# Weight tiles of a retention and FFN kernel converted in pairs: twenty of 32 in operations of 1024 columns

## The chip, the cores and the metric

The kernel runs on one core of a Trainium2 chip. A core has five engines that run side by side, each in the order of its own program: TensorE (PE, matrix products), VectorE (DVE), ScalarE (ACT), GpSimd (POOL) and SyncE (SP, which here starts the DMA transfers). They wait for each other by semaphores. The metric is the time of one execution in microseconds (us).

## The reference

Eight batches of 576 tokens with eight heads of 64 go through a retention (attention with a decay in place of a softmax). Its output is the input x of a feed-forward layer with a rational function between two products:

```python
gamma = 1.0 - 2.0 ** (-5.0 - np.arange(H))
Dmat = np.where(rel >= 0, gamma[:, None, None] ** rel, 0.0)   # rel = i - j
ret = (scale * q @ k.T * Dmat) @ v
x = ret.transpose(0, 2, 1, 3).reshape(B * S, H * D)            # 4608 x 512
h = x @ w_in                                                    # 512 x 2048
P = a[0] + a[1] * h + a[2] * h2 + a[3] * h3
Q = 1.0 + abs(b[0]) * abs(h) + abs(b[1]) * h2
out = (P / (Q + 1e-06)) @ w_out                                 # 2048 x 512
```

w_in and w_out come as 64-bit floats, the rest as 32-bit ones.

## The kernel before

The tokens are cut into 36 units of 128, worked off in "visits" of 64x64 matmuls, and into nine blocks b of 512 for the feed-forward layer; its hidden columns into 16 tiles f of 128. A step is one (b, f). It runs `gemm1` (h{b}_{f} = x times a tile of w_in, 12 matmuls of 512 columns), the rational function on ScalarE and VectorE (tiles p, u, v, named p{b}_{f} and so on; in steps 8 to 20 u lies in a spare PSUM tile called free_at), the split of the result into g hi and g lo, and three or four steps later `gemm2` (acc += g times a tile of w_out, 12 matmuls). The order of steps is block 0 with f 0 to 7, block 1 with all 16, block 0 with f 8 to 15, then blocks 2 to 8. Twelve matmuls stand for four because each fp32 operand is a sum of a hi and a lo part, and three of the four products are taken.

Each of the 32 weight tiles (128 x 512, 16 of w_in called i0 to i15, 16 of w_out called o0 to o15) is converted from its 64 bits on the chip, in five instructions: on ScalarE c <- the high words of bits and bits <- the low words (both read every other 32-bit word), on VectorE an stt (scalar_tensor_tensor: shift and or) that joins them in c, on ScalarE w hi <- c, and on VectorE or GpSimd w lo = c - w hi. The tiles o0 to o3 lie in `held` tiles and are used whole at first; their w hi comes late, from step 7 on, and reads every other word of `held`.

PSUM (the memory that matmuls write) holds two buffers for h, so the gemm1 of step i+2 waits until the instruction p2 of step i (`ffn_p2`, on VectorE) has read the first h. The results of block 0's first half are moved out of PSUM by the two evictions o0_0 and o0_1 on ScalarE (1024 columns each), which the first gemm2 of block 1 waits for.

Everything is written out by hand and kept in that order on each engine: the lists FIRST0 to FIRST23, MID, DENSE, DENSE_ALONE and REST name the parts of a step in the order in which they are recorded (split0 to split3 are the four points at which conversions under way go on by one instruction, `start` begins new ones), and further lists say for every step or tile which engine does a part: VA and SCALES, SCALES_Q, LO, WLO. All recorded instructions bear the line number of the recording helper, L86, so that rows of the trace are told apart by the names of tiles.

Of the kernel before, what the change touches and what calls it, by code (L numbers as in the profile page):

```python
# [21 lines left out]
P = 128  # L22
# [15 lines left out]
FIRST0 = "gemm1 split0 start ffn_r visit split3 decay decay1 ffn_p ffn_q ffn_va ffn_v gemm2 ffn_p2 keep_hi add split1 keep_lo ffn_hi split2 ffn_lo scale_v fade scale_q ffn_q3".split()  # L38
FIRST1 = "gemm1 visit split1 ffn_r ffn_p decay scale_q keep_hi scale_v split0 ffn_p2 decay1 ffn_va add ffn_q split3 ffn_q3 start ffn_v ffn_hi split2 fade keep_lo gemm2 ffn_lo".split()
FIRST2 = "start ffn_hi gemm1 scale_q visit ffn_lo decay ffn_p keep_hi decay1 add split2 ffn_va ffn_p2 scale_v fade ffn_r ffn_q split3 gemm2 split1 ffn_v keep_lo ffn_q3 split0".split()  # L40
FIRST3 = "split3 gemm2 ffn_hi start gemm1 ffn_r visit decay split1 split0 ffn_p decay1 add scale_v keep_hi ffn_va ffn_q split2 scale_q ffn_v keep_lo ffn_q3 fade ffn_lo ffn_p2".split()
FIRST4 = "gemm1 split0 ffn_p gemm2 split3 ffn_p2 visit scale_q ffn_r ffn_va decay decay1 start keep_hi ffn_q split2 split1 ffn_hi ffn_q3 add fade ffn_v keep_lo scale_v ffn_lo".split()
FIRST5 = "scale_q ffn_hi gemm1 split3 scale_v visit split0 decay decay1 add start ffn_p gemm2 keep_hi ffn_r ffn_va split1 fade ffn_v ffn_q ffn_p2 ffn_q3 split2 ffn_lo keep_lo".split()
FIRST6 = "ffn_r gemm1 split0 split3 gemm2 ffn_p visit ffn_hi decay keep_hi scale_v split1 ffn_lo decay1 split2 start ffn_va add ffn_q fade ffn_q3 keep_lo ffn_v ffn_p2 scale_q".split()
FIRST7 = "scale_v ffn_hi start gemm1 ffn_p visit keep_hi split0 ffn_p2 ffn_va decay ffn_lo ffn_v gemm2 decay1 add split3 ffn_r ffn_q keep_lo ffn_q3 scale_q split1 split2 fade".split()
FIRST21 = "visit gemm1 gemm2 scale_v split1 decay decay1 ffn_p add keep_hi ffn_r ffn_va ffn_hi keep_lo start ffn_lo split2 ffn_p2 ffn_q ffn_q3 ffn_v split0 fade scale_q split3".split()
FIRST22 = "split1 scale_v visit gemm1 scale_q ffn_p keep_hi keep_lo decay ffn_va ffn_hi ffn_r start decay1 ffn_lo ffn_q gemm2 ffn_p2 split2 add split0 ffn_v fade ffn_q3 split3".split()
FIRST23 = "start split3 scale_q split2 gemm1 visit ffn_p ffn_hi ffn_r decay ffn_p2 ffn_q keep_hi split1 decay1 keep_lo ffn_q3 add ffn_va ffn_v split0 gemm2 scale_v fade ffn_lo".split()
MID = "split2 gemm1 start ffn_p split0 ffn_p2 ffn_r gemm2 ffn_hi ffn_va ffn_v ffn_q ffn_q3 ffn_lo split3 split1".split()
DENSE = "scale_q split0 gemm1 ffn_p ffn_hi visit keep_hi split2 decay ffn_va ffn_v scale_v decay1 split3 ffn_lo ffn_r ffn_q gemm2 ffn_q3 add ffn_p2 split1 fade keep_lo".split()  # L50
DENSE_ALONE = "split2 split0 gemm1 visit split1 gemm2 scale_q ffn_p ffn_r decay ffn_p2 keep_hi decay1 ffn_q add ffn_hi ffn_lo keep_lo fade split3 ffn_va ffn_v scale_v ffn_q3".split()
# [38 lines left out]
def retention_ffn(ctx: ExitStack, tc: tile.TileContext, qkv, w_in, w_out, consts, masks, out):  # L90
# [17 lines left out]
    cnv = ctx.enter_context(tc.tile_pool(name="cnv", bufs=4))  # L108
# [15 lines left out]
    def load_unit(n):  # L124


        late = 2 <= n < 6
        pools = [(wts, f"w{w}_{10 + n}") if late else (raw, "qk" if w == 0 else "kv") for w in range(2)]
        qk = pools[0][0].tile([P, 2, NPAIR, P], F32, tag=pools[0][1], name=f"qk{n}")
        nc.sync.dma_start(qk, qkv[n, :, 0:1024].rearrange("p (a g i) -> p a g i", a=2, g=NPAIR))  # L130
        kv = pools[1][0].tile([P, 2, H, D], F32, tag=pools[1][1], name=f"kv{n}")
# [30 lines left out]
    plain, held = {}, []  # L162
    step = -1

    def load_weight(k):

        bits[k] = wts.tile([P, DM], I64, tag=f"w{k[0]}_{k[1]}", name=f"bits{k[0]}_{k[1]}")
        nc.sync.dma_start(bits[k], (w_in, w_out)[k[0]][k[1]])

    def split_weight(k):  # L170


        nm = f"{k[0]}_{k[1]}"
# [22 lines left out]
        while late and step < PLAIN_TO + PLAIN.index(str(k[1])):  # L196
            yield
        w = wts.tile([P, 2, DM], F32R, tag=f"w{nm}", name=f"w{nm}")
        del bits[k]
        if late:  # L200
            cf = cf.rearrange("p (n a) -> p a n", a=2)
        halved = [w[:, i, :].rearrange("p (a n) -> p a n", a=2) if late else w[:, i, :] for i in range(2)]
# [377 lines left out]
    def gemm2(b, f, first, last):  # L580
# [42 lines left out]
    def put_last(b, t, acc):  # L623

        if t != 2:
            pool_, tag, n = (op, "o0", 2) if t == 0 else (cnv, "c", 1)
            lasts.append(pool_.tile([P, n, DM], F32, tag=tag, name=f"last{t}"))
# [3 lines left out]
        def store_rows(queue, a, tiles, o):  # L631
            queue.dma_start(rows[a][:, tiles], o[a::2])
# [107 lines left out]
    for i in range(len(steps) + lag(len(steps))):  # L740
# [28 lines left out]
        load_weights(2)  # L769
# [42 lines left out]
```

## Time and profile before

| | us |
|---|---|
| three runs | 866.65, 869.79, 869.87 (median 869.79) |
| the profiled execution | 866.07 |
| its span, from the first to the last instruction | 864.3 |
| TensorE busy | 844.1 (98%) |
| VectorE busy | 760.1 (88%) |
| ScalarE busy | 670.1 (78%) |
| GpSimd busy | 127.4 (15%) |

The busy times are sums over the whole span. The conversion of weights lies in the first fifth of it, where the shares are others; the rows below show them by stretch.

### The profile page before, as it was taken

Reading aid. Unit: us, or ns where it says so; the run is one execution under the profiler, and the core shown is the slowest. Engines: PE = TensorE matmul, PEld = TensorE weight load, DVE = VectorE, ACT = ScalarE, POOL = GpSimd, SP = SyncE. Lnnn points to the kernel's source line nnn. Section 1 sums busy time; section 2 is a strip of 40 time slices with the busy share of each in tenths; the row PEclk is TensorE's granted clock in tenths of the full one; section 3 lists DMA queues with packets and bytes.
Section 4 is the critical chain, followed back from the end, with each engine's and each line's share of the span. In section 5 each row is a group of like instructions: output and inputs, shape, how many; then the busy total and the mean of one; then the engine's idle time right before and its main releaser. Section 6 shows DMA issues by size and latency. Waiting matters only on the chain.

```text
span 864.3 us, 18728 instructions
## 1 busy us (share of the span) xinstructions
PE 844.1 (98%) x7574; PEld 727.1 (84%) x7574; DVE 760.1 (88%) x1222; ACT 670.1 (78%) x1234; POOL 127.4 (15%) x105
## 2 busy tenths in 40 slices
PE   8799899999999999999999999999999999999997
PEld 6667788888888888888888888888888888888886
DVE  4999989999988888888888888898888998888995
ACT  3998999997777778777877787778777787767774
POOL 4411344230001110111111110001111111000000
PEclk9999999999999999999999999999999999999999
DMA  9994000033111112111211121111201121001001
GB/s 343 358 351 188 1 2 0 2 135 112 38 71 41 50 50 99 50 50 50 98 50 50 49 99 50 49 49 47 77 31 46 50 99 50 1 2 49 1 1 49
DMA packets 20773, 64.54 MB, mean 75 GB/s; under 512 B 2512, under 2 KB 2640, under 8 KB 20688
## 3 DMA queue, kind: packets, MB, share of 16 engines
q1 hardware_dynamic: 20528, 63.10, 20.7%
q8 instruction: 59, 0.97, 0.5%
q14 instruction: 26, 0.21, 0.1%
q10 hardware_dynamic: 160, 0.26, 0.1%
HBM read 53.91 MB, written 9.44 MB: 73 GB/s over the span
## 4 chain that ended last, share of the span: by engine, by line
PE 87%; ACT 8%; issue 2%; DVE 2%; DMA 0%; POOL 0%; SPq 0%; DVEq 0%; ACTq 0%; POOLq 0%
PE acc L86 40%; PE h L86 39%; PE ps L86 4%; PE y L86 2%; ACT free_at L86 2%; ACT c L86 1%; PE psNone L86 1%; ACT p L86 1%; ACT w L86 1%; ACT g L86 1%; DMA qk<-in_qkv 0%; ACT v L86 0%; DVE kv L86 0%; PE ps_None L86 0%; DVE p L86 0%
## 5 line engine op out<-in xcount | busy, mean ns | idle before, releaser
L86 PE MATMUL acc<-w,g 128*128 128x512 f32 x1584 | 368.1, 382 | 2.9 <-ACT o L86 2.2
L86 PE MATMUL h<-xhi,w 128*128 128x512 f32 x1152 | 366.8, 380 | 2.6 <-DVE p L86 1.2
L86 PEld LDWEIGHTS acc<-w,g 128*128 128x128 f32 x1584 | 297.9, 190 | 47.2 <-ACT o L86 2.6
L86 PEld LDWEIGHTS h<-xhi,w 128*128 128x128 f32 x1152 | 217.7, 189 | 34.8 <-DVE p L86 1.6
L86 ACT ACTIVATE p<-h,const_sb 128x512 f32<-128x512 f32 x144 | 111.5, 774 | 160.0 <-PE h L86 159.8
L86 PE MATMUL h<-xlo,w 128*128 128x512 f32 x576 | 218.4, 379 | 1.0 <-DVE xlo L86 1.0
L86 DVE TENSOR_TENSOR p<-p,h 128x512 f32<-128x512 f32 x144 | 98.7, 685 | 50.6 <-ACT u L86 47.7
L86 PEld LDWEIGHTS h<-xlo,w 128*128 128x128 f32 x576 | 108.9, 189 | 17.1 <-DVE xlo L86 1.3
L86 DVE SCALAR_TENSOR_TENSOR p<-p,const_sb,h 128x512 f32<-128x512 f32 x144 | 107.4, 746 | 3.9
L86 POOL TENSOR_TENSOR S<-S,const_sb 128x256 f32<-128x256 f32 x32 | 37.3, 1166 | 462.3 <-DVE S L86 431.8
L86 ACT ACTIVATE v<-u,absb 128x512 f32<-128x512 f32 x128 | 102.6, 801 | 0.1
L86 DVE SCALAR_TENSOR_TENSOR p<-v,p 128x512 f32<-128x512 f32 x140 | 97.9, 700 | 3.7
L86 DVE SCALAR_TENSOR_TENSOR p<-p,const_sb,u 128x512 f32<-128x512 f32 x131 | 98.2, 749 | 0.5 <-ACT u L86 0.5
L86 DVE TENSOR_TENSOR v<-v,u 128x512 f32<-128x512 f32 x130 | 90.1, 693 | 1.7 <-ACT v L86 1.7
L86 DVE SCALAR_TENSOR_TENSOR v<-v,u 128x512 f32<-128x512 f32 x131 | 89.9, 686 | 0.0
L86 ACT ACTIVATE u<-u 128x512 f32<-128x512 f32 x131 | 82.8, 632 | 4.2
L86 ACT ACTIVATE g<-p 128x512 fp32r<-128x512 f32 x132 | 82.7, 626 | 3.3 <-DVE p L86 3.1
L86 ACT ACTIVATE u<-v 128x512 f32<-128x512 f32 x131 | 82.0, 626 | 1.8 <-DVE v L86 1.8
L86 DVE TENSOR_TENSOR g<-p,g 128x512 fp32r<-128x512 f32 x114 | 78.1, 685 | 0.7 <-ACT g L86 0.7
L86 ACT ACTIVATE u<-h 128x512 f32<-128x512 f32 x131 | 76.8, 586 | 1.0 <-DVE v L86 0.9
L86 ACT ACTIVATE kv<-kv,const_sb 128x64 f32<-128x64 f32 x224 | 56.2, 335 | 0.0
L86 POOL TENSOR_TENSOR qk<-qk,const_sb 128x512 f32<-128x512 f32 x32 | 43.7, 1366 | 45.0 <-DMA qk<-in_qkv 45.0
(95 smaller groups left out, 701.3 us busy)
## 6 DMA issues: line engine op xcount, KB each, us to landing
qk<-in_qkv SPq DMA_DIRECT2D x36, 512.0 KB, 4.2
kv<-in_qkv SPq DMA_DIRECT2D x32, 512.0 KB, 5.6
bits<-in_w_in SPq DMA_DIRECT2D x16, 512.0 KB, 9.0
bits<-in_w_out SPq DMA_DIRECT2D x16, 512.0 KB, 9.3
out<-o SPq DMA_DIRECT2D x28, 256.0 KB, 3.1
kv<-in_qkv SPq DMA_DIRECT2D x4, 256.0 KB, 7.2
out<-o SPq DMA_DIRECT2D x8, 128.0 KB, 2.1
out<-last SPq DMA_DIRECT2D x2, 256.0 KB, 2.4
```

The costliest lines, as they stand in the source:

```text
L86: return lambda *a, **k: self.tc.keep_in_program_order(method(*a, **k))
```

## The change

Twenty of the 32 tiles are converted two at a time: the list GROUPS names twelve single tiles (the first eleven, and o13, which stands between the last two pairs) and ten pairs. A pair is loaded into one tile of 128 x 2 x 512 and goes through c, bits and the stt in one instruction of 1024 columns each, and through w hi in one of 2 x 512; w lo stays one instruction a tile. The pool `cnv` has two buffers of 1024 columns instead of four of 512, and two single tiles share one. The loads are spread over the steps by a list LOADW instead of two a step, four early units are loaded into the space of the last four pairs, and the output of block 1 leaves from one tile of two halves. All the lists of order and of engines are new. TensorE's matmuls are the same; two visits (in steps 4 and 6) stand ahead of that step's gemm2 now.

```diff
-STARTS = "1 2 1 2 2 0 1 0 1 0 1 1 1 1 1 1 2 1 1 2 1 1 1 1".split()
+STARTS = "1 1 2 1 1 1 0 0 1 1 0 1 0 1 1 1 0 1 1 1 0 0 0 0".split()
+GROUPS = "i0 i1 i2 i3 o0 i4 o1 i5 o2 i6 o3 i7,o4 o5,o6 o7,i8 i9,i10 i11,o8 i12,o9 i13,o10 i14,o11 i15,o12 o13 o14,o15".split()
-MID = "split2 gemm1 start ffn_p split0 ffn_p2 ffn_r gemm2 ffn_hi ffn_va ffn_v ffn_q ffn_q3 ffn_lo split3 split1".split()
+MID = "split3 start gemm1 split0 split1 ffn_p ffn_p2 ffn_r ffn_hi ffn_va ffn_q ffn_v ffn_q3 split2 gemm2 ffn_lo".split()
+LOADW = "4 0 1 2 0 2 1 0 0 0 1 1 1 0 3 3 0 0 0 2".split()
...
-    cnv = ctx.enter_context(tc.tile_pool(name="cnv", bufs=4))
+    cnv = ctx.enter_context(tc.tile_pool(name="cnv", bufs=2))
...
+    def load_weight(g):
+
+        bits[g] = wts.tile([P, len(groups[g]), DM], I64, tag=f"w{g}", name=f"bits{g}")
+        for i, (w, f) in enumerate(groups[g]):
+            nc.sync.dma_start(bits[g][:, i], (w_in, w_out)[w][f])
...
-            c = cnv.tile([P, DM], I32, tag="c", name=f"c{nm}")
-            cf = c.bitcast(F32)
+            if n == 2 or not shared:
+                shared[:] = [cnv.tile([P, 2 * DM], F32, tag="c", name=f"c{g}")]
+                flat = shared[0][:, 0 : n * DM]
+                if n == 2:
+                    shared.clear()
+            else:
+                flat = shared.pop()[:, DM:]
+        c, cf = flat.bitcast(I32), flat.rearrange("p (f c) -> p f c", f=n)
-        act.activation(cf, high.bitcast(F32), AF.Prelu, scale=math.ldexp(1.0, -112), alpha=-math.ldexp(1.0, 32))
+        act.activation(flat, high.bitcast(F32), AF.Prelu, scale=math.ldexp(1.0, -112), alpha=-math.ldexp(1.0, 32))
         act.activation(packed, low.bitcast(U32), AF.Copy, scale=math.ldexp(7.49, -32))
...
-        act.activation(halved[0], cf, AF.Copy)
-        engine = dve if WLO[len(parts)] == "vector" else pool
-        engine.tensor_tensor(halved[1], cf, halved[0].bitcast(F32), ALU.subtract)
-        parts[k] = w
+        act.activation(whole[:, :, 0], cf, AF.Copy)
+        for i, k in enumerate(groups[g]):
+            engine = dve if WLO[len(parts)] == "vector" else pool
+            engine.tensor_tensor(whole[:, i, 1], cf[:, i], whole[:, i, 0].bitcast(F32), ALU.subtract)
+            parts[k] = both[:, i]
...
-        load_weights(2)
+        load_weights(int(LOADW[i]) if i < len(LOADW) else 0)
```

Where the lists move instructions is seen in the order of the engines' programs. The first place is ScalarE around the two evictions o0_0 and o0_1 (written o0_0_7 and o0_1_7; the last number of a name only tells tiles apart). Before:

```order
L86 ACTIVATE g1_0_1163<-p1_0_1050 128x512
L86 ACTIVATE w1_3_1171<-held1_414 128x512
L86 ACTIVATE c0_9_1192<-bits0_9_853 128x512
L86 ACTIVATE bits0_9_853<-bits0_9_853 128x512
L86 ACTIVATE p1_3_1196<-h1_3_1179,const_sb_95 128x512
L86 ACTIVATE free_at_1032<-h1_3_1179 128x512
L86 ACTIVATE free_at_1032<-v1_2_1143 128x512
L86 ACTIVATE free_at_1032<-free_at_1032 128x512
L86 ACTIVATE o0_0_7_1215<-acc0_0_0_670 128x1024
L86 ACTIVATE o0_1_7_1217<-acc0_0_1_671 128x1024
L86 ACTIVATE g1_1_1219<-p1_1_1090 128x512
```

The same place in the changed kernel, where c15 and bits15 are the c and bits of the pair i11,o8 (a group's number in GROUPS, counted from 0, stands in place of a tile's):

```order
L88 ACTIVATE g1_0_1121<-p1_0_1026 128x512
L88 ACTIVATE c15_1144<-bits15_867 128x1024
L88 ACTIVATE bits15_867<-bits15_867 128x1024
L88 ACTIVATE p1_3_1162<-h1_3_1147,const_sb_95 128x512
L88 ACTIVATE free_at_1000<-h1_3_1147 128x512
L88 ACTIVATE free_at_1000<-v1_2_1113 128x512
L88 ACTIVATE free_at_1000<-free_at_1000 128x512
L88 ACTIVATE g1_1_1169<-p1_1_1066 128x512
L88 ACTIVATE o0_0_7_1188<-acc0_0_0_670 128x1024
L88 ACTIVATE o0_1_7_1190<-acc0_0_1_671 128x1024
```

A pair stands where one tile stood, the late w hi (w1_3 before) has moved further ahead, and g1_1 has passed from behind the evictions to ahead of them.

The second place is VectorE at the end of the start, around the last xlo that the first gemm1 reads. Before:

```order
L86 TENSOR_TENSOR xlo0_194<-psNone_2_215,xhi0_193 128x4x128
L86 TENSOR_TENSOR S4_332<-S3_276,early_110 128x256
L86 TENSOR_TENSOR w0_1_340<-c0_1_271,w0_1_340 128x512
L86 TENSOR_TENSOR xlo0_194<-psNone_3_305,xhi0_193 128x4x128
L86 TENSOR_TENSOR qk4_244<-psNone_4_360,mask_sb_96 128x512
L86 TENSOR_TENSOR qk5_252<-qk5_252,const_sb_95 128x512
```

And in the changed kernel, where w0 is the tile i0 (w0_1 above is i1):

```order
L88 TENSOR_TENSOR xlo0_192<-psNone_2_213,xhi0_191 128x4x128
L88 TENSOR_TENSOR S4_326<-S3_271,early_110 128x256
L88 TENSOR_TENSOR w0_331<-c0_264,w0_331 128x512
L88 TENSOR_TENSOR xlo0_192<-psNone_3_300,xhi0_191 128x4x128
L88 TENSOR_TENSOR both4_242<-psNone_4_354,mask_sb_96 128x512
L88 TENSOR_TENSOR both5_249<-both5_249,const_sb_95 128x512
```

VectorE's w lo ahead of the last xlo is that of tile i0 now, and GpSimd does that of i1; before it was the other way round.

## Rows read from the trace of the kernel before

**Rows 1.** Stretches: busy time (and instructions) of each engine, clock, DMA share, GB/s.

```profile
40.00:73.00 33.00, 30.03 (x304) 19.89 (x295) 31.39 (x55) 30.25 (x55) 4.05 (x4) 1.00 0.94 359
73.50:98.80 25.30, 24.20 (x112) 20.66 (x110) 24.70 (x39) 24.67 (x39) 8.24 (x6) 1.00 0.09 32
98.80:153.20 54.40, 51.43 (x228) 44.11 (x228) 50.22 (x76) 53.48 (x85) 22.22 (x18) 0.97 0.00 1
176.00:850.00 674.00, 673.23 (x6052) 586.97 (x6051) 597.66 (x967) 508.56 (x969) 67.08 (x51) 1.00 0.16 54
```

The engines stand in the order PE, PE's weight loads, VectorE, ScalarE, GpSimd.

**Rows 2.** Waits of TensorE: us in total, times, longest.

```profile
PE ps L86 <- issue: 2.8, 1, 2.8
PE acc L86 <- ACT o L86: 2.2, 1, 2.2
...
PE h L86 <- DVE p L86: 1.2, 1, 1.2
...
PE h L86 <- DVE xlo L86: 1.0, 1, 1.0
PE h L86 <- DVE kv L86: 0.7, 1, 0.7
...
PE h L86 <- ACT v L86: 0.7, 1, 0.7
```

**Rows 3.** Stretch behind the wait for o (columns as in rows 1).

```profile
100.30:103.60 3.30, 3.30 (x9) 2.62 (x8) 3.27 (x5) 3.27 (x6) 1.28 (x1) 0.50 0.00 0
```

**Rows 4.** Timeline of TensorE: start, us, operation, idle before and its releaser.

```profile
92.36 2.75 PE L86 MATMUL acc<-w,g 128*128 128x512 f32 x12
...
99.91 4.54 PE L86 MATMUL acc<-w,g 128*128 128x512 f32 x12 [2.21 <-ACT o L86]
```

**Rows 5.** Timeline of ScalarE, pieces from p0_7 to behind o0_0.

```profile
74.35 0.76 ACT L86 ACTIVATE p<-h,const_sb 128x512 f32<-128x512 f32 x1
...
79.54 0.78 ACT L86 ACTIVATE p<-h,const_sb 128x512 f32<-128x512 f32 x1 [0.28 <-PE h L86]
...
87.33 0.78 ACT L86 ACTIVATE v<-free_at,absb 128x512 f32<-128x512 f32 x1
88.00 0.87 ACT L86 ACTIVATE w<-held 128x512 fp32r<-128x512 f32 x1
88.77 0.62 ACT L86 ACTIVATE w<-c 128x512 fp32r<-128x512 f32 x1
89.29 0.87 ACT L86 ACTIVATE c<-bits 128x512 f32<-128x512 f32 x1
90.19 0.89 ACT L86 ACTIVATE bits<-bits 128x512 int32<-128x512 uint32 x1
90.99 0.77 ACT L86 ACTIVATE p<-h,const_sb 128x512 f32<-128x512 f32 x1
...
98.84 1.94 ACT L86 ACTIVATE o<-acc 128x1024 f32<-128x1024 f32 x2
100.65 0.64 ACT L86 ACTIVATE g<-p 128x512 fp32r<-128x512 f32 x1
101.17 0.64 ACT L86 ACTIVATE w<-c 128x512 fp32r<-128x512 f32 x1
101.69 0.69 ACT L86 ACTIVATE c<-bits 128x512 f32<-128x512 f32 x1
```

**Rows 6.** Groups of instructions by shape, first 230 us: busy us, mean ns, idle before.

```profile
L86 ACT ACTIVATE c<-bits 128x512 f32<-128x512 f32 x28 | 22.8, 815 | 0.0
...
L86 ACT ACTIVATE o<-acc 128x512 f32<-128x512 f32 x4 | 2.0, 594 | 0.0
...
L86 ACT ACTIVATE o<-acc 128x1024 f32<-128x1024 f32 x2 | 1.9, 1024 | 0.0
```

**Rows 7.** Timeline of VectorE, the w lo ahead of the last xlo and that xlo.

```profile
25.30 1.78 DVE L86 TENSOR_TENSOR w<-c,w 128x512 fp32r<-128x512 f32 x1 [0.76 <-ACT w L86]
27.00 0.68 DVE L86 TENSOR_TENSOR xlo<-psNone,xhi 128x512 fp32r<-128x512 f32 x1
```

**Rows 8.** DMA queues from 40 to 42 us: packets, MB, share of 16 engines.

```profile
q8 instruction: 1, 0.02, 2.7%
```

More of the change, by code (lines that the diff above doesn't have):

```diff
@@ L51 @@
-DENSE_ALONE = "split2 split0 gemm1 visit split1 gemm2 scale_q ffn_p ffn_r decay ffn_p2 keep_hi decay1 ffn_q add ffn_hi ffn_lo keep_lo fade split3 ffn_va ffn_v scale_v ffn_q3".split()
+FIRST0 = "ffn_r gemm1 split2 ffn_p gemm2 visit split3 ffn_q scale_q ffn_q3 keep_hi scale_v ffn_hi decay decay1 ffn_p2 add ffn_va ffn_lo start fade split1 ffn_v split0 keep_lo".split()
+FIRST1 = "visit split1 gemm1 ffn_r ffn_p ffn_hi decay ffn_p2 decay1 ffn_lo ffn_q scale_v ffn_va split2 start add keep_hi scale_q ffn_q3 keep_lo ffn_v gemm2 fade split0 split3".split()
@@ new lines @@
+FIRST2 = "gemm1 visit ffn_p decay ffn_va ffn_r ffn_v split1 ffn_q start ffn_hi split2 decay1 gemm2 split3 keep_hi ffn_p2 split0 add keep_lo scale_q fade ffn_lo ffn_q3 scale_v".split()
+FIRST3 = "scale_q ffn_r visit gemm2 keep_hi split3 split0 decay ffn_hi gemm1 ffn_p ffn_p2 ffn_q scale_v ffn_va split1 split2 ffn_q3 decay1 start keep_lo ffn_v add fade ffn_lo".split()
+FIRST4 = "split2 scale_v gemm1 ffn_p visit start split1 split3 decay decay1 ffn_hi ffn_r add ffn_va ffn_v ffn_q ffn_q3 fade gemm2 keep_hi keep_lo split0 scale_q ffn_p2 ffn_lo".split()
@@ new lines @@
+FIRST5 = "split3 split0 gemm1 ffn_r visit scale_q decay ffn_p decay1 ffn_q keep_hi ffn_p2 keep_lo add ffn_va ffn_hi split1 fade scale_v ffn_lo ffn_v gemm2 ffn_q3 start split2".split()
+FIRST6 = "gemm1 split2 visit split0 ffn_p decay ffn_r ffn_q keep_hi ffn_q3 scale_v split3 ffn_hi ffn_p2 decay1 ffn_va add ffn_lo scale_q fade gemm2 ffn_v split1 start keep_lo".split()
+FIRST7 = "visit ffn_hi gemm1 keep_hi split3 decay scale_v ffn_p split0 scale_q gemm2 ffn_r ffn_q ffn_p2 decay1 ffn_va split1 ffn_lo ffn_q3 split2 ffn_v add start keep_lo fade".split()
@@ new lines @@
+FIRST21 = "start visit gemm1 split0 decay split2 ffn_p ffn_p2 ffn_hi keep_hi gemm2 decay1 add split1 ffn_lo keep_lo fade ffn_va scale_q ffn_r ffn_q split3 scale_v ffn_q3 ffn_v".split()
+FIRST22 = "gemm1 scale_q start split0 visit split1 ffn_p decay keep_hi split3 ffn_hi decay1 scale_v add fade ffn_r split2 gemm2 ffn_p2 ffn_q keep_lo ffn_lo ffn_va ffn_v ffn_q3".split()
+FIRST23 = "gemm1 split2 scale_v visit split3 ffn_p decay ffn_r keep_hi scale_q decay1 gemm2 split1 ffn_va ffn_hi ffn_p2 add ffn_q ffn_q3 ffn_v start keep_lo split0 fade ffn_lo".split()
@@ L52 @@
+MID = "split3 start gemm1 split0 split1 ffn_p ffn_p2 ffn_r ffn_hi ffn_va ffn_q ffn_v ffn_q3 split2 gemm2 ffn_lo".split()
+DENSE = "gemm1 visit scale_q decay ffn_hi split1 ffn_p decay1 ffn_p2 ffn_r ffn_lo ffn_va ffn_v scale_v ffn_q keep_hi add ffn_q3 gemm2 split2 split3 split0 fade keep_lo".split()
+DENSE_ALONE = "split1 visit split2 gemm1 ffn_r ffn_p ffn_q ffn_hi decay ffn_p2 decay1 ffn_q3 ffn_va split3 split0 ffn_lo ffn_v gemm2 add keep_hi keep_lo scale_q fade scale_v".split()
 REST = (
@@ L127, in load_unit @@
         late = 2 <= n < 6
-        pools = [(wts, f"w{w}_{10 + n}") if late else (raw, "qk" if w == 0 else "kv") for w in range(2)]
-        qk = pools[0][0].tile([P, 2, NPAIR, P], F32, tag=pools[0][1], name=f"qk{n}")
+        if late:
+            both = wts.tile([P, 2, DM * 2], F32, tag=f"w{wide[n - 2]}", name=f"both{n}")
+            qk = both[:, 0].rearrange("p (a g i) -> p a g i", a=2, g=NPAIR)
+            kv = both[:, 1].rearrange("p (a h d) -> p a h d", a=2, h=H)
+        else:
+            qk = raw.tile([P, 2, NPAIR, P], F32, tag="qk", name=f"qk{n}")
+            kv = raw.tile([P, 2, H, D], F32, tag="kv", name=f"kv{n}")
         nc.sync.dma_start(qk, qkv[n, :, 0:1024].rearrange("p (a g i) -> p a g i", a=2, g=NPAIR))
-        kv = pools[1][0].tile([P, 2, H, D], F32, tag=pools[1][1], name=f"kv{n}")
         a = 1 if n < NP else 0
@@ L195, in split_weight @@
         yield
-        while late and step < PLAIN_TO + PLAIN.index(str(k[1])):
+        while late and step < PLAIN_TO + PLAIN.index(str(f)):
             yield
-        w = wts.tile([P, 2, DM], F32R, tag=f"w{nm}", name=f"w{nm}")
-        del bits[k]
+        both = wts.tile([P, n, 2, DM], F32R, tag=f"w{g}", name=f"w{g}")
+        del bits[g]
+        whole = both
         if late:
-            cf = cf.rearrange("p (n a) -> p a n", a=2)
-        halved = [w[:, i, :].rearrange("p (a n) -> p a n", a=2) if late else w[:, i, :] for i in range(2)]
-        act.activation(halved[0], cf, AF.Copy)
-        engine = dve if WLO[len(parts)] == "vector" else pool
-        engine.tensor_tensor(halved[1], cf, halved[0].bitcast(F32), ALU.subtract)
-        parts[k] = w
+            cf, whole = cf.rearrange("p f (n a) -> p f a n", a=2), both.rearrange("p f j (a n) -> p f j a n", a=2)
+        act.activation(whole[:, :, 0], cf, AF.Copy)
[3 more added lines that the diff above has]
+            parts[k] = both[:, i]
     xs = {}
@@ L604, in gemm2 @@
             if b == 1:
+                both = cnv.tile([P, 2, DM], F32, tag="c", name=f"o{b}_{t}")
                 for j in range(2):
-                    o = cnv.tile([P, 1, DM], F32, tag="c", name=f"o{b}_{t}_{j}")
-                    act.activation(o[:, 0], acc[:, j, :], AF.Copy, scale=-1.0)
-                    store(b, 2 * t + j, o)
+                    act.activation(both[:, j], acc[:, j, :], AF.Copy, scale=-1.0)
+                    store(b, 2 * t + j, both[:, j : j + 1])
                 continue
@@ L625, in put_last @@
         if t != 2:
-            pool_, tag, n = (op, "o0", 2) if t == 0 else (cnv, "c", 1)
-            lasts.append(pool_.tile([P, n, DM], F32, tag=tag, name=f"last{t}"))
+            pool_, tag = (op, "o0") if t == 0 else (cnv, "c")
+            lasts.append(pool_.tile([P, 2, DM], F32, tag=tag, name=f"last{t}"))
         act.activation(lasts[-1][:, t == 2, :], acc, AF.Copy, scale=-1.0)
@@ L631, in store_rows @@
         def store_rows(queue, a, tiles, o):
-            queue.dma_start(rows[a][:, tiles], o[a::2])
+            queue.dma_start(rows[a][:, tiles], o[a::2, 0 : len(range(*tiles.indices(4)))])
         if t == 2:
@@ L659, in lag @@
         return 4 if NF // 2 <= i < first - 2 or i >= len(steps) - 8 else 3
-    need = [((at[1, f] if f >= half else f) + 3 * w, w, f) for w in range(2) for f in range(NF)]
-    order = [(w, f) for _, w, f in sorted(need)]
-    loads, splits = iter(order), iter(order)
+    groups = [[("io".index(x[0]), int(x[1:])) for x in g.split(",")] for g in GROUPS]
+    wide = [g for g, names in enumerate(groups) if len(names) == 2][-4:]
+    loads, splits = iter(range(len(groups))), iter(range(len(groups)))
     going = []
```

43 lines of the change are left out of this document (14 added, 29 removed).

## Prediction

> **What bounds the kernel now.** I read the table of stretches first [rows 1]. From 176 us on, TensorE is busy for 673.2 of 674.0 us, so that four fifths of the program have nothing to give: the change leaves TensorE's work as it is. All that can move lies before. There VectorE and ScalarE are nearly full as well: from 73.5 to 98.8 us ScalarE works 24.67 of 25.30 us and VectorE 24.70, and from 98.8 to 153.2 us ScalarE works 53.48 of 54.40 while TensorE stands still for 3.0. The view of waits says what TensorE stood still for [rows 2]. Its large waits after the first twenty-odd microseconds are 2.84 us of issue, 2.2 for ScalarE's o, 1.23 for VectorE's p, 1.04 for xlo, 0.7 for kv and 0.7 for v: 8.7 us together. One cost stands in no wait: behind the wait for o the granted clock is 0.50, the lower of the two levels (1.2 GHz), for about 3.4 us [rows 3], and the twelve matmuls of acc that start at 99.91 take 4.54 us, where the twelve at 92.36 took 2.75 [rows 4]. That is 1.8 more, so that 10.5 us, or 1.2%, is the most that this change can win.
>
> Then I followed ScalarE from instruction to instruction [rows 5]. The distance from one start to the next is what an instruction costs when the engine is full: c 0.90, bits 0.80, g and w hi 0.52 each, late w hi 0.77, v 0.67, o of 1024 columns 0.90. The eviction o0_0 starts at 98.84, and TensorE goes on 1.07 later, at 99.91. Between p0_7 (74.35) and o0_0 ScalarE waits once for 0.28; the rest of the 24.49 us is work. The end of the eviction is therefore set by how much is queued on ScalarE ahead of it.
>
> **What a pair costs.** No row shows c or bits over 1024 columns, so they are bounded. The lower bound takes from the row of o what 512 more columns cost: 1.024 against 0.594, which is 0.43 [rows 6]. That gives c 0.90 + 0.43 = 1.33 and bits 1.23. The upper bound adds what a read with a stride costs: late w hi, which reads every other word, lasts 0.87 to 0.88 where w hi lasts 0.62 [rows 5], 0.26 more, and c and bits read every other word too. So 512 columns more cost up to 0.69: c 1.59, bits 1.49. A pair of c and bits thus costs 2.56 to 3.08, where two single ones take 3.40. The w hi of a pair reads and writes in a row: 0.52 + 0.43 = 0.95 against 1.04. Ten pairs save 4.1 to 9.3 us of ScalarE's time, and on VectorE (1.14 by the same argument against 2 x 0.60) 0.6.
>
> The row of single c operations speaks for the upper half: they last 815 ns on average where o of the same 512 columns lasts 594 [rows 6], and the one at 101.69, under the half clock, lasts 0.69 [rows 5]; a cost that falls when TensorE runs slower is not a fixed one, and so would double. The Trainium skill (ScalarE: Activation LUTs, What ACT_TABLE_LOAD costs) gives an ACTIVATE with immediate operands 186 ns and 0.833 ns for each column, whatever it reads: 613 ns and 1039 ns, as an estimate from that page, for 512 and 1024. The w and o rows agree with it and the c row, at 815, does not; by the page a pair of c and bits would cost some 2.1 us. I take the middle of the two bounds, 2.82.
>
> **What the change moves.** Saved time counts only where ScalarE is late, and there the order brings work forward. Counted in the order of both kernels, 37 instructions stand on ScalarE from p0_7 to o0_0 in each. The tiles whose c and bits stand there are 3 before (three singles, 5.10 us) and 6 after (three pairs, 7.68 to 9.24): +2.58 to +4.14. w hi: two singles become three pairs, +1.81. g1_1 stood behind the evictions and stands ahead of them now, +0.52 (the evictions themselves move with nothing: what they write is stored only with the second half of the block). One v goes to VectorE, -0.67, and one of the four late w hi stands ahead of p0_7 now, -0.77. Sum: +3.47 to +5.03.
>
> p0_7 itself should come earlier. The first gemm1 waited 1.04 for xlo [rows 2], because VectorE had a w lo queued ahead of xlo that itself waited 0.76 for ScalarE and then lasted 1.78, beside GpSimd's own w lo [rows 7]. Now that w lo is of the first tile, whose hi part is a ScalarE instruction earlier. I take 1.04 as won. The wait for issue, 2.84, I leave where it is: at its end one transfer of 16 KB on the instruction queue shows [rows 8], while the DMA engines are 0.94 busy over the stretch [rows 1], and the change alters neither the length of TensorE's program ahead of it nor the bytes loaded.
>
> So p0_7 starts at 74.35 - 1.04 = 73.31, o0_0 at 73.31 + 24.49 - 0.28 + 3.47 = 100.99 up to 102.55, and TensorE goes on at 102.06 to 103.62: 2.15 to 3.71 later than before, with the same fall of the clock behind it.
>
> From o0_0 to p1_11 ScalarE had 45.29 us of work. There the tiles are 10 singles before and 5 pairs and a single after: 17.0 against 14.5 to 17.1 for c and bits, w hi nine at 0.52 against five at 0.95 and one at 0.52 (+0.6), one g less (-0.5). That is -2.4 to +0.2. The wait of 1.23 for VectorE's p stands where that stretch ends (it waits for the p2 of p1_11, and p1_11 is a ScalarE instruction); so it goes at the low end and is 0.2 longer at the high end. The wait of 0.66 for v lies two steps on, where all 32 tiles are through and ScalarE has a slack of some us a step; it goes in both cases. Behind it TensorE is full. Low end: +2.15 - 1.23 - 0.66 = +0.3. High end: +3.71 + 0.2 - 0.66 = +3.3. Middle: +1.8.
>
> The other parts cost nothing that shows. Loads: the same 32 tiles and 36 units, with the DMA share already 0.94; the share falls to 0.09 in the stretch from 73.5 us, so the later ones have room. The w lo that go to GpSimd are covered, since it is busy for 8.24 of 25.30 us [rows 1]; without that cover one costs VectorE 0.6. The output tile of block 1 moves the same bytes.
>
> **The sum.** The profiled execution of before took 866.07 us, with a span of 864.3; the changed one should take 867.9. The three runs shown have a mean of 868.77, 2.7 above the profiled one, and a median of 869.79. I add the 2.7: 870.6.
>
> **Rivals.**
> *Cheap pairs.* If what c and bits cost above an o is paid once for an operation, and falls to what the c at 101.69 shows (0.69 where the c at 89.29 lasted 0.87 [rows 5], 0.18 less), a pair costs 2.56 - 2 x 0.18 = 2.20. Then the three pairs take 6.60, o0_0 comes 1.08 earlier than at the low end, at 99.9, TensorE goes on 1.07 later than before, and the waits of 1.23 and 0.66 go: -0.8, or 868.0. For it speaks that w and o fit one slope; against it the average of 815. It is inside what counts as no change. The Trainium skill's rule cited above (ScalarE: Activation LUTs) would be this case. Chance 0.15.
> *Faster.* The issue wait of 2.84 doesn't come again, since the transfer on the instruction queue happens to fall between other loads, in an order of loads that is new. TensorE and p0_7 are then 2.8 earlier, o0_0 comes at 98.2 to 99.7, TensorE goes on as early as before or earlier, and with ScalarE caught up the clock falls for less. Middle: 870.6 - 2.8 - 1.8 = 866.0; with cheap pairs as well 863. Against it: the place in TensorE's program is the same, and the queues are as full. Chance 0.18.
> *Slower: VectorE becomes the bound.* Between p0_7 and o0_0 it has 0.6 us to spare [rows 1]. It gets one more v (0.84) and three more tiles there, and its stt of a pair must wait until c and bits of both tiles are done, 2.8 us where it was 1.7. Counted with 0.60 an operation of 512 columns and 1.14 for a pair, VectorE's work from the first xlo to p1_7 is 91.7 against 88.0: +3.7 that nothing hides if its few idle moments stay where they are. TensorE's h has two buffers and needs the p2 of two steps before, so this lands on TensorE: it adds to the 2 to 4 us of the eviction whatever VectorE is later than ScalarE, some 2 to 3. That gives +4.5 to +6, 874 to 875. It decides from the point where o0_0 starts after 104. For it: VectorE has over 97% in that stretch; against it: from p1_11 on the order gives VectorE less. Chance 0.17.
> *The change is neutral as forecast*: 0.50.
>
> **How the numbers follow.** The likeliest case says 870.6, with a range of its own of 868 to 873 (the two bounds and a microsecond for runs). To hold 8 in 10 the range takes in most of the faster and the slower rival: 865.0 to 875.0. A difference of 0.5% (4.3 us) is about what a measurement of this kernel tells from none. Faster by more needs 865.4 or less: nearly the best half of the faster rival, and a combination of cheap pairs with fewer stalls, 0.18. Slower by more needs 874.1: most of the slower rival, 0.16. The rest, 0.66, is no difference.
>
> **What would show it.** Right: no wait for xlo ahead of the first gemm1; pairs of c and bits starting 1.3 to 1.6 apart; o0_0 between 100.5 and 103, and behind it the clock at 0.50; no wait of 0.66 for v; ScalarE below 90% from 160 us on; TensorE over 99% from 176 us on. Wrong: o0_0 before 99 or after 104, TensorE waiting for VectorE's p at several steps from p1_1 on, an issue wait of another size, or a new wait of TensorE in the visits that now stand ahead of gemm2.

## The result and the profile after

The changed kernel took 874.54 us (median of six runs, 871.48 to 875.46), the kernel before 869.45 in the same measurements (six runs, 866.65 to 871.38). The ratio is 1.0051, with a 95% interval of 1.0033 to 1.0069: the change costs about 0.5%. The profiled execution took 871.91, with a span of 869.9 against 864.3, 5.6 us more. The six times of the changed kernel fall into two groups (871.48 and 871.91; 874.09 to 875.46), and the profiled executions lie 2.6 us (changed) and 3.4 us (before, 866.07) below the medians, so that shares read from one profile each, as those below, hold to some 3 us.

The same stretches as in [rows 1], with the same columns; p0_7 starts at 76.06 now and o0_0 at 105.50:

```profile
40.00:73.00 33.00, 29.95 (x353) 19.84 (x353) 29.58 (x50) 28.12 (x42) 6.39 (x6) 1.00 0.94 346
76.06:105.50 29.44, 24.02 (x108) 19.75 (x106) 29.30 (x41) 28.50 (x37) 10.93 (x8) 1.00 0.01 4
...
176.00:850.00 674.00, 673.23 (x6169) 586.91 (x6168) 599.65 (x966) 507.73 (x967) 65.24 (x51) 1.00 0.16 54
```

Behind 176 us TensorE is as full as before, to the hundredth. The loss is made ahead of it. From p0_7 to o0_0 the kernel before took 24.49 us; now it is 29.44, and VectorE works 29.30 of them and ScalarE 28.50. TensorE's waits, in answer to [rows 2]:

```profile
PE h L88 <- DVE p L88: 6.7, 7, 2.6
PE acc L88 <- ACT o L88: 3.2, 1, 3.2
PE ps L88 <- issue: 2.5, 2, 2.2
...
PE y L88 <- issue: 1.7, 1, 1.7
...
PE h L88 <- DVE both L88: 1.0, 1, 1.0
```

The wait for VectorE's p (the p2 that frees a buffer of h) was 1.23 us, once; it is 6.7 us in seven places. The wait for o has grown from 2.2 to 3.2. The issue wait has become three: 1.65 and 0.23 in the visit of step 2, and a new one of 2.22 in that of step 4. The wait for xlo is gone, and that of v as well; the one for kv, a tile that is called both now, has grown from 0.70 to 1.04. Three of the places on TensorE's timeline, in answer to [rows 4] (the lowest row is the first gemm2 of block 1):

```profile
55.24 0.27 PE L88 MATMUL ps<-kv 64*64 64x64 f32 x2 [2.22 <-issue]
...
95.38 0.48 PE L88 MATMUL h<-xhi,w 128*128 128x512 f32 x1 [2.60 <-DVE p L88]
...
106.57 2.86 PE L88 MATMUL acc<-w,g 128*128 128x512 f32 x12 [3.15 <-ACT o L88]
```

What ScalarE did between p1_0 and p1_1, and around o0_0, in answer to [rows 5]:

```profile
86.73 1.04 ACT L88 ACTIVATE w<-c 128x1024 fp32r<-128x1024 f32 x1
87.68 1.55 ACT L88 ACTIVATE c<-bits 128x1024 f32<-128x1024 f32 x1
89.25 1.59 ACT L88 ACTIVATE bits<-bits 128x1024 int32<-128x1024 uint32 x1
90.75 0.76 ACT L88 ACTIVATE p<-h,const_sb 128x512 f32<-128x512 f32 x1
...
104.98 0.62 ACT L88 ACTIVATE g<-p 128x512 fp32r<-128x512 f32 x1
105.50 1.93 ACT L88 ACTIVATE o<-acc 128x1024 f32<-128x1024 f32 x2
```

From start to start c costs 1.57, bits 1.50 and the w hi of a pair 0.95. And the groups by shape, in answer to [rows 6]:

```profile
L88 ACT ACTIVATE bits<-bits 128x1024 int32<-128x1024 uint32 x10 | 15.5, 1548 | 0.3
L88 ACT ACTIVATE c<-bits 128x1024 f32<-128x1024 f32 x10 | 14.7, 1465 | 0.0
...
L88 ACT ACTIVATE o<-acc 128x1024 f32<-128x1024 f32 x2 | 1.9, 1023 | 0.0
```

Where the 5.6 us come from can be added up along the steps. On ScalarE p0_7 starts 1.71 later than before. o0_0 follows 4.95 later still (29.44 against 24.49). From there to TensorE's gemm1 of h1_14 it is 0.4 more (that gemm1 starts at 160.27 against 153.23, 7.04 in all): the waits for p there are 3.3 us instead of 1.2, there is no wait for v, and no stretch at the lower clock, 1.2 GHz (half clock below). Behind it 1.4 come back, 0.9 of them in the next full visit (2.09 us against 2.99).

### The profile page after: what moved, and what is told of

Read it like the earlier page. It is cut to its first block, busy times and chain, and to the rows that moved or that the text cites. A ratio compares the mean times of both kernels' runs of the same rounds, so it can differ in the third digit from the quotient of the medians.

```text
span 869.9 us, 18679 instructions
## 1 busy us (share of the span) xinstructions
PE 844.0 (97%) x7574; PEld 725.6 (83%) x7574; DVE 763.9 (88%) x1208; ACT 664.9 (76%) x1194; POOL 135.6 (16%) x112
## 4 chain that ended last, share of the span: by engine, by line
PE 86%; ACT 7%; DVE 4%; issue 2%; DMA 1%; POOL 0%; SPq 0%; DVEq 0%; ACTq 0%; POOLq 0%
PE acc L88 40%; PE h L88 38%; PE ps L88 4%; PE y L88 2%; ACT c L88 1%; PE psNone L88 1%; ACT free_at L88 1%; DVE p L88 1%; ACT w L88 1%; ACT p L88 1%; ACT bits L88 1%; DVE c L88 1%; ACT g L88 1%; DMA qk<-in_qkv 1%; DVE v L88 0%
## 5 line engine op out<-in xcount | busy, mean ns | idle before, releaser
L88 POOL TENSOR_TENSOR S<-S,const_sb 128x256 f32<-128x256 f32 x32 | 33.7, 1055 | 456.8 <-DVE S L88 416.5
L88 DVE SCALAR_TENSOR_TENSOR p<-p,const_sb,u 128x512 f32<-128x512 f32 x131 | 100.5, 767 | 0.5 <-ACT u L88 0.5
L88 DVE TENSOR_TENSOR v<-v,u 128x512 f32<-128x512 f32 x130 | 93.3, 717 | 1.0 <-ACT v L88 1.0
L88 ACT ACTIVATE kv<-kv,const_sb 128x64 f32<-128x64 f32 x216 | 54.2, 334 | 0.0
```

The source lines that it names most:

```text
L88: return lambda *a, **k: self.tc.keep_in_program_order(method(*a, **k))
```

## The experiments

The comparisons are with the kernel before, timed together with each run; times "from p0_7 to p1_14" are ScalarE's, from the profile of each kernel (85.30 us before, 89.21 after the change).

**The pairs taken apart.**

```diff
-        act.activation(flat, high.bitcast(F32), AF.Prelu, ...)
-        act.activation(packed, low.bitcast(U32), AF.Copy, ...)
+        for r in cuts:
+            act.activation(flat[:, r], high[:, r].bitcast(F32), AF.Prelu, ...)
+            act.activation(packed[:, r], low[:, r].bitcast(U32), AF.Copy, ...)
```

(`cuts` holds the ranges of 512 columns, two for a pair; stt and w hi likewise.) 

> The changed kernel with every pair taken apart again: c, bits, stt and w hi are two instructions of 512 columns each, in the same place of the same order. Theory: pairing itself saves a little (measured 1.57 + 1.55 + 0.95 us for a pair of c, bits and w hi against 2 x 2.22 for singles, 0.37 a pair), and what was lost is the order that brings conversions forward. Then o0_0 starts 1.5 to 2 us later than in the changed kernel (four to five pairs ahead of it) and the time is 1 to 3 us longer. Rival: long instructions block p and u behind them and are themselves the loss; then o0_0 comes earlier and the time falls by 1 to 5 us.

Measured: ratio 1.0044 (1.0026 to 1.0063), median 873.37. From p0_7 to p1_14 it takes 90.69 us, 1.5 more than the changed kernel with its eight pairs there, 0.2 a pair; o0_0 comes 0.5 later behind p0_7. So a pair saves something, less than the 0.37 reckoned, and in the time it doesn't show (the interval holds the changed kernel's 1.0051). Long instructions are not the loss, and the pairing is hardly a gain: what moved the time is in the rest of the change, of which the order is taken up next.

**The visit of step 4 behind gemm2 again.**

```diff
-FIRST4 = "split2 scale_v gemm1 ffn_p visit start ... fade gemm2 keep_hi ..."
+FIRST4 = "split2 scale_v gemm1 ffn_p gemm2 visit start ... fade keep_hi ..."
```

> The changed kernel with one row moved: in step 4 gemm2 (four plain matmuls a tile row) stands ahead of the visit again, as it did before. Theory: the issue wait of 2.22 us in that visit comes of TensorE reaching its many small instructions too early after the last visit; with 3.6 us of matmuls ahead of it the wait shrinks to under 0.5, p0_7 starts about 2 us earlier, and the time falls by 1 to 2.2 us (less than all, since ScalarE and VectorE are full behind it). Rival: the wait belongs to the visit wherever it stands or to the loads of that moment; then it stays near 2 us and the time is the same.

Measured: ratio 1.0015 (1.0002 to 1.0028), median 870.05. The wait of 2.22 is gone, one of 0.70 for kv has come behind the visit, p0_7 starts at 74.41 instead of 76.06, p1_14 at 163.49 instead of 165.27, and the span is 868.1 instead of 869.9. The 1.7 us that p0_7 wins pass to the end whole, where a part was expected to be lost.

By the timed runs the move is worth more than by these two profiles: the ratio falls from 1.0051 to 1.0015, 0.36% or 3.1 us, with intervals that don't meet. Three other kernels that leave the visit ahead of gemm2, timed together with this one, have 1.0042, 1.0044 and 1.0064 (below and above). So the place of this one visit is the larger part of the loss; where the share beyond 1.8 us arises, no trace shows.

In the profile after, TensorE stops at 53.0 in the middle of the visit's small matmuls, and a transfer of 16 KB on the instruction queue starts at 52.9 and takes 0.92:

```profile
q1 hardware_dynamic: 191, 0.70, 102.9%
q8 instruction: 1, 0.02, 2.9%
```

(DMA queues of the changed kernel from 52 to 54 us: packets, MB, share of 16 engines.) With gemm2 ahead of the visit the same transfer starts at 52.13, while TensorE works on gemm2. The Trainium skill (Runtime: NRT & Kernel Launch, Instruction fetch mechanics) says that an engine's instructions are fetched in pieces of 16 KiB, the next while the current one runs. The rows agree as far as they go: such a packet of 16 KB lies in the issue waits of 2.84 (before) and 2.22, and TensorE goes on 1.38 and 1.41 us after it has landed (41.81 to 43.19, and 53.83 to 55.24). In eleven of the 13 profiles here an issue wait in these visits ends so, 1.25 to 1.47 us after the end of such a transfer. The wait of 1.65 doesn't: it is over 0.2 before its transfer is. That TensorE waits for its next instructions there is thus supported; why the transfer starts when it does was not tested.

**The same move in the kernel before.**

```diff
-FIRST4 = "gemm1 split0 ffn_p gemm2 split3 ffn_p2 visit scale_q ..."
+FIRST4 = "gemm1 split0 ffn_p split3 ffn_p2 visit gemm2 scale_q ..."
```

> The kernel before with gemm2 of step 4 behind the visit, as the changed kernel has it, and nothing else. Theory, the place of the visit makes the issue wait: a second issue wait of about 2 us appears in that visit beside the first of 2.84, p0_7 comes 1 to 2 us later, and the time is 1 to 2 us longer. Rival, the wait comes of the changed loads: no second wait, and the time is the same.

Measured: ratio 1.0059 (1.0041 to 1.0077), median 873.86. The move costs more than expected, and by another wait than expected: no second issue wait, but one for VectorE's p, since a visit takes one of the two buffers of h for its y:

```profile
58.29 0.37 PE L86 MATMUL y<-qk 64*64 64x64 f32 x2 [2.51 <-DVE p L86]
```

and the clock falls behind it (stretch from 58.3 to 65.5, columns as in [rows 1]):

```profile
58.30:65.50 7.20, 7.20 (x87) 4.44 (x88) 6.45 (x13) 4.95 (x9) 2.71 (x3) 0.56 0.73 222
```

p0_7 starts at 82.61 here, 8.3 later than in the profile of before; from p0_7 to p1_14 it takes 85.20 us, as before, and the span is 8.1 longer. So what is lost ahead of p0_7 passes on whole in this kernel too. Not all of the 8.3 is the move's: the issue wait ahead of the moved visit is 3.71 in this profile instead of 2.84, and half clock follows it until 47.7. By the medians the move costs 5 us.

**The evictions ahead of p1_3.**

```diff
+MID_O = "split3 start gemm1 split0 split1 gemm2 ffn_p ..."
-... else MID if free_at else ...
+... else MID_O if i == 11 else MID if free_at else ...
```

> The changed kernel with gemm2 of step 11 recorded ahead of p, so that the two evictions o0_0 and o0_1 stand ahead of p1_3 on ScalarE. Theory that ScalarE's queue ahead of the evictions is what TensorE waits for there: o0_0 starts about 2.9 us earlier, the wait for o falls from 3.15 to under 0.5, and the time falls by 1 to 3 us. Rival, VectorE or ScalarE as a whole sets the pace: p1_3 and its p2 come 1.8 us later, a wait for p appears within the next three gemm1 that gives back what was won, and the time is the same within 1 us.

Measured: ratio 1.0042 (1.0025 to 1.0059), median 872.1. The wait for o is gone, and from p0_7 to p1_14 it takes 89.15 us against 89.21: the rival is right. A wait of 1.87 for p has appeared at 125.56. The wait for o is a place where a late ScalarE shows, no loss of its own.

**One pair begun a step later.**

```diff
-STARTS = "1 1 2 1 1 1 0 0 1 1 0 1 0 1 1 1 0 1 1 1 ..."
+STARTS = "1 1 2 1 1 1 0 0 1 1 0 0 1 1 1 1 0 1 1 1 ..."
```

> The changed kernel with the pair i11,o8 begun one step later (behind the evictions, where it is still three steps ahead of its first use). Theory, conversions brought forward are the loss: ScalarE has 3.1 us less ahead of o0_0, which starts about 102.4 to 103, the wait for o falls under 0.6, and the time falls by 2 to 4 us. Rival, the work is only put off: waits for p at h1_9 to h1_13, 3.3 us now, grow by about 3, and the time is the same within 1 us.

Measured: ratio 1.0064 (1.0046 to 1.0082), median 874.54. The gemm2 behind o0_0 comes 29.42 us behind p0_7 instead of 30.51, and its wait for o is 0.35; but new waits for p of 1.80 and 1.17 follow at 128.67 and 135.29, and p1_14 comes 91.16 us behind p0_7, 2.0 later than in the changed kernel. The work is only put off.

**Four pairs begun sooner, and the evictions early as well.** On top of the kernel with gemm2 ahead of the visit:

```diff
-STARTS = "1 1 2 1 1 1 0 0 1 1 0 1 0 1 1 1 0 1 1 1 ..."
+STARTS = "1 1 2 1 1 1 1 0 1 0 1 0 1 0 1 1 0 1 1 1 ..."
```

> e2_visit4 with four pairs begun earlier: o7,i8 by two steps (ahead of p0_7, where ScalarE is idle 1.4 us now), i9,i10, i11,o8 and i12,o9 by one. Theory, the stretch from p0_7 to p1_11 is over-full on ScalarE and VectorE (15 tiles converted in it before p1_14 by the kernel before, 17 by the changed one) and idle time ahead of it was left unused: p0_7 comes up to 1.7 later, one pair of c and bits fewer but one w hi more stands between p0_7 and o0_0, and p1_11 starts 1 to 3 us earlier after the start of the step; time 1 to 2.5 us less. Rival, VectorE has no room for the earlier stt and w lo either: p1_11 moves by less than 0.7 and the time is the same.

> e11_pair_sooner with the evictions o0_0 and o0_1 ahead of p1_3, as in e3_o_early. Theory: the wait for o is gone (3.15 to under 0.5), but as ScalarE's total work up to p1_11 is the same, the time is within 1 us of e11_pair_sooner, with fewer stretches of half clock. Rival: the wait for o was a loss of its own; then the time is 1.5 to 3 us below e11_pair_sooner, and no longer above the kernel before.

Measured: ratios 1.0073 (1.0053 to 1.0094) and 1.0068 (1.0046 to 1.0089), medians 875.95 and 875.59: both are slower than the kernel they start from. p0_7 comes 3.1 later, and ScalarE now waits where it did not (waits of ScalarE from 50 to 165 us in the first of the two):

```profile
ACT free_at L89 <- DVE v L89: 3.0, 5, 2.1
ACT w L89 <- DVE c L89: 2.8, 1, 2.8
...
ACT c L89 <- DVE w L89: 1.5, 1, 1.5
```

w hi waits for an stt that VectorE has not reached, and the next c for a w lo that holds one of the two buffers for pairs. Neither the theory nor the rival of the first held: VectorE has no room for the earlier conversions, as the rival had it, but the time grew instead of staying. That early evictions change nothing, the theory of the second, was borne out again.

**c and bits without the stride.** Again on top of the kernel with gemm2 ahead of the visit:

```diff
+        low = bits[g].bitcast(I32).rearrange("p f w -> p (f w)")[:, 0 : n * DM]
+        high = const_sb[:, 0:DM].unsqueeze(1).broadcast_to([P, n, DM])
-        act.activation(flat, high.bitcast(F32), AF.Prelu, ...)
+        act.activation(flat.rearrange("p (f c) -> p f c", f=n), high, AF.Prelu, ...)
```

> e2_visit4 with c reading a constant tile and bits reading their words in a row instead of every other word (the weights that come out are not those of the reference; every instruction, shape and order stays). Theory, the read with a stride is what c and bits cost more: a pair of them lasts about 1.03 us each, as the o of 1024 columns does, instead of 1.47 and 1.55; ScalarE loses 1 us a pair from p0_7 on, and the time falls by 1 to 4 us as far as VectorE lets it. Rival, c and bits last longer because of their function or the 32-bit integers they read: they stay near 1.5.

Measured: ratio 0.9962 (0.9951 to 0.9973), median 865.6. The two groups (columns as in [rows 6]):

```profile
L89 ACT ACTIVATE c<-const_sb 128x1024 f32<-128x1024 f32 x10 | 10.5, 1047 | 0.0
L89 ACT ACTIVATE bits<-bits 128x1024 int32<-128x1024 uint32 x10 | 10.5, 1047 | 0.0
```

The stride is the surcharge: 1.05 instead of 1.47 and 1.55, and 0.62 for one tile instead of 0.73 and 0.76. From p0_7 to p1_14 it takes 84.88 us, 4.2 less. The estimate from the Trainium skill (ScalarE: Activation LUTs, What ACT_TABLE_LOAD costs), 1039 ns, is right for such a read (1047). For every other word, of which that section says nothing, it is 0.43 and 0.51 us too low. Whether the pairs would gain anything over single tiles read in a row was not run.

**bits left out for three pairs.** On top of the same kernel:

```diff
-        act.activation(packed, low.bitcast(U32), ...)
+        if 13 <= g <= 15:
+            packed = c
+        else:
+            act.activation(packed, low.bitcast(U32), ...)
```

> e2_visit4 without the bits instruction of three pairs (o7,i8; i9,i10; i11,o8), whose stt reads c twice instead (those six tiles come out wrong). ScalarE has 4.7 us less between p0_7 and o0_0, VectorE has the same. Theory, ScalarE's queue sets that stretch: o0_0 starts 3 to 4.7 us earlier and the time falls by 2 to 4 us. Rival, VectorE sets it: o0_0 starts less than 1.5 earlier, waits of h for p stay, and the time falls by less than 1 us.

Measured: ratio 0.9996 (0.9981 to 1.0011), median 868.7. ScalarE has 4.6 us less to do from p0_7 to o0_0, and the stretch shrinks by 1.8, from 29.39 to 27.60:

```profile
73.78:101.38 27.60, 24.01 (x108) 19.75 (x106) 27.49 (x39) 23.89 (x35) 11.89 (x8) 1.00 0.01 2
```

(columns as in [rows 1]; in the kernel it starts from, VectorE works 29.25 and ScalarE 28.45 of 29.39.) This is between the two expectations: with ScalarE relieved, VectorE is full, 27.49 of 27.60, and sets the pace. ScalarE works 23.89 us in it, about as much as before the change (23.86 from p0_7 to o0_0), yet the stretch is 3.1 longer than the 24.49 before: so much VectorE's new work takes by itself.

**Four w lo moved to GpSimd.**

```diff
-WLO = "vector pool pool pool vector pool pool vector vector vector vector pool vector vector vector ..."
+WLO = "vector pool pool pool vector pool pool vector vector vector pool pool pool pool pool ..."
```

> e2_visit4 with four w lo (of o1, o6, o2 and o7) moved from VectorE to GpSimd, between p0_7 and p1_1. Theory, VectorE's queue between p1_1 and its p2 sets the pace there: VectorE has 2.7 us less ahead of the p2 that h1_3 waits for, the wait of 2.60 falls under 0.6, o0_0 starts 1.5 to 2.5 us earlier and the time falls by 1 to 2.5 us. Rival, ScalarE sets it: o0_0 starts within 0.7 of where it did and the time is the same within 0.7 us.

Measured: ratio 1.0033 (1.0019 to 1.0046), median 871.7. It went the other way: from p0_7 to o0_0 it takes 30.56 us instead of 29.39. Neither theory has that, and the timelines show why. VectorE, and below it GpSimd:

```profile
78.35 1.78 DVE L89 SCALAR_TENSOR_TENSOR p<-p,const_sb,u 128x512 f32<-128x512 f32 x1
80.05 1.76 DVE L89 SCALAR_TENSOR_TENSOR v<-v,u 128x512 f32<-128x512 f32 x1
81.74 0.73 DVE L89 SCALAR_TENSOR_TENSOR p<-p,const_sb,h 128x512 f32<-128x512 f32 x1
...
87.58 1.87 DVE L89 SCALAR_TENSOR_TENSOR p<-p,const_sb,u 128x512 f32<-128x512 f32 x1
89.38 1.77 DVE L89 SCALAR_TENSOR_TENSOR v<-v,u 128x512 f32<-128x512 f32 x1
```

```profile
78.27 1.31 POOL L89 TENSOR_TENSOR w<-held,w 128x512 fp32r<-128x512 f32 x1 [4.06 <-ACT w L89]
79.53 3.41 POOL L89 TENSOR_TENSOR w<-c,w 128x512 fp32r<-128x512 f32 x2
...
87.60 1.30 POOL L89 TENSOR_TENSOR w<-held,w 128x512 fp32r<-128x512 f32 x1
88.86 1.73 POOL L89 TENSOR_TENSOR w<-c,w 128x512 fp32r<-128x512 f32 x1
```

While GpSimd works on a w lo, VectorE's instructions on two tiles of SBUF last 1.8 us instead of 0.7, and GpSimd's own 1.7 instead of 1.3. Six instructions of 512 columns or less are stretched so between p0_7 and o0_0, by 5.6 us together, where the changed kernel has two (1.5 us) and the kernel before none. The four w lo taken from VectorE were worth 2.7, by the expectation. The Trainium skill (SBUF — State Buffer, Who interferes with whom) says that VectorE and GpSimd share a pair of ports under an exclusive lock, and that the loser waits; the rows fit that, and they also show both as the loser.

**The first three w lo alone, in the kernel before.**

```diff
-WLO = "pool vector vector pool vector ..."
+WLO = "vector pool pool pool vector ..."
```

> The kernel before with nothing but the engines of the first three w lo taken from the changed kernel (i0 on VectorE, i1 and i2 on GpSimd). Theory, what TensorE wins or loses ahead of p0_7 passes to the end almost whole: the wait for xlo (1.04) ahead of the first gemm1 goes, p0_0 starts 1 to 1.9 us earlier, p0_7 0.5 to 1.2 earlier, and the time is 0.5 to 1.2 us less, at the edge of what five rounds tell. Rival: the next wait (0.7 for kv, 2.84 for issue) takes it back; p0_7 moves by less than 0.3 and the time is the same.

Measured: ratio 0.9987 (0.9973 to 1.0001), median 868.09 against 868.85. The wait for xlo is gone, but the expectation failed in the steps behind it: p0_0 starts at 31.79, 0.35 later than before and not 1 to 1.9 earlier, and TensorE reaches the visit of step 2 at 38.17 against 38.21, so that in this profile next to nothing of the 1.04 is left there. Then an issue wait of 3.15, with half clock until 50 us, puts p0_7 at 77.90, so its share can't be read. It is the best of the kernels here that compute the reference, by 0.1% with an interval that just reaches one; so no version is shown to be faster than the kernel before.

## Why the prediction was right and where it failed

The time lay in the range, 3.9 us above the likeliest value and 0.5 below the upper end, thanks to the width of the range; all four signs named for being wrong came. Of the cases, not the likeliest (+1.8 us, 870.6) happened but the slower one, which had been given 0.17: o0_0 starts at 105.50, beyond the 104 from which it decides, and TensorE waits for VectorE's p at seven steps. The loss, 5.1 us by the medians, lies just past the 4.3 at which "no difference" was to end. Step by step:

*p0_7 at 74.35 - 1.04.* This step failed, by 2.75 us. The wait for xlo went as said, but 1.04 was not won by it: the wait for kv behind it grew by 0.34, and TensorE reaches the visit of step 2 at 37.73 against 38.21, 0.5 earlier. (p0_0 starts 1.85 earlier, mostly because it stands ahead of four other instructions on ScalarE now.) The issue wait was left "where it is" because the program ahead of it was as long; in that visit it shrank from 2.84 to 1.88. Its transfer, taken to lie at the end of the wait, ran from 40.93 to 41.81, in the middle of it. But the visit of step 4, which had moved ahead of gemm2, was priced at nothing, and it met an instruction transfer of its own: 2.22 us. Putting gemm2 back removed it and gave 1.8 us of span, and 3.1 by the timed runs. That is shown for this kernel; in the kernel before the same move costs too, by another wait.

*The price of a pair.* The bounds held, and the upper one was the truth: 1.57 + 1.50 for c and bits between starts, against 1.59 + 1.49. The argument from the strided w hi gave it; taking the middle was the mistake, and the reason given for the upper half should have been followed. The fall of c under the half clock, which was read as a sign, proved nothing: without the stride nothing of the surcharge is left. At the upper price the prediction's own sum is its high end, +3.3.

*From p0_7 to o0_0: +3.47 to +5.03 on ScalarE.* Measured 29.44 - 24.21 = +5.23. The tally of ScalarE was right (it works 4.64 more), and its top was passed by 0.2, while ScalarE waits for VectorE for 0.6 at 97.2. What the path left out is VectorE, whose work in the stretch grew by 5.4, from 23.89 to 29.30 us; the prediction had it in the slower rival alone, with 3.7 over a longer stretch.

*From o0_0 to p1_11: -2.4 to +0.2.* Measured 46.60 against 45.41, +1.2. A sum over ScalarE alone no longer holds here: bits left out of three pairs gave back only 1.8 of 4.6 us. VectorE and ScalarE hand the chain to each other, as the rival had it.

*The waits.* The one for v went, as said; that for p at h1_13 is 1.32 (the high end, 1.23 + 0.2, said 1.43). The half clock behind the wait for o was taken as given and did not come in this profiled execution. That it would have cost 1.8 is not shown: the last section has a case in which it cost nothing.

*What the edits that "cost nothing" cost.* Loads and the two buffers of `cnv`: nothing seen; no c and no w hi of ScalarE waits in the changed kernel from 20 to 165 us. The w lo on GpSimd: "covered, since it is busy for 8.24 of 25.30 us" was the wrong question. GpSimd had time, but its w lo stretched two of VectorE's instructions by 1.5 us between p0_7 and o0_0; [rows 7] had shown such a one, 1.78 us, and the prediction used it only for the start.

*The rivals.* "Faster" needed the issue wait to go; it split and grew. "Cheap pairs" is refuted by 1.47 and 1.55, and the run without the stride shows what it would have been worth: 4.2 us up to p1_14. The slower rival's size (+4.5 to +6, which on 868.8 is 873.3 to 874.8 and not quite the 874 to 875 stated) was right, its cause only in part: of the 5.6 us of span the visit has 1.8 (by the timed runs 3.1 of 4.4). Of the longer stretch from p0_7 to o0_0 VectorE would make 3.1 us alone, as the run without bits shows; what ScalarE would make alone was not run, since relieving VectorE failed.

## What to carry to other kernels

Before two instructions are joined, find out whether they cost by the instruction or by the element: here a third of the price of c and bits is the stride, which is paid for every element, and joining saved 0.2 us a pair. Where two engines are both over 95% busy, count both, and count as one resource what they share: work moved from VectorE to GpSimd came back as stretched instructions on VectorE. And price every row that a new order moves on TensorE, those of many small matmuls first, even if the sum of work is the same.

## What the runs showed that was not expected

The half clock does not follow each wait. The changed kernel and the one with gemm2 ahead of the visit have the same wait of 2.60 at the same gemm1 (95.38 and 93.72), and behind it (columns as in [rows 1]) first the changed kernel, then the other:

```profile
95.50:98.80 3.30, 3.30 (x16) 2.90 (x17) 3.27 (x5) 2.64 (x5) 3.30 (x3) 1.00 0.02 5
```

```profile
93.80:97.10 3.30, 3.30 (x9) 2.65 (x10) 3.30 (x5) 2.64 (x5) 3.30 (x3) 0.58 0.02 5
```

In the changed kernel's profile none of the waits of 2.22, 2.60 and 3.15 brought the level of 1.2 GHz. In the kernel before one of 2.84 did not and one of 2.21 did. In the kernel before with the visit moved two stretches of it stood ahead of p0_7, one behind the issue wait of 3.71 and one of 7 us at the wait of 2.51 in the moved visit.

Nor does a half clock always cost time. Behind the 2.60 it slowed TensorE in the second kernel, but as it is busy for 1.7 us longer from p0_7 to o0_0 (25.70 against 24.02), the wait for o that follows is shorter by as much, 1.43 instead of 3.15:

```profile
104.87 2.86 PE L89 MATMUL acc<-w,g 128*128 128x512 f32 x12 [1.43 <-ACT o L89]
```

From p0_7 to p1_14 the two take 89.21 and 89.08 us: where VectorE and ScalarE set the pace, TensorE only waited less. The times of the changed kernel don't follow the clock either. Its mean granted clock was 1.000 in the profiled execution and 0.994 to 0.998 in the other five, so that half clock came in each of those; yet 871.48 us has 0.995 and 875.46 has 0.998. What decides whether such a stretch comes, and what parts the executions, stays open.
